# Top-k attention with a feed-forward block: the scores of a row folded in two before the top 32 are selected

## The chip, the cores and the metric

The kernel runs on one core of a Trainium2 chip. The metric is the device time of one execution in microseconds (us). The core has five engines that work side by side, each with its own queue in program order: TensorE (PE, matrix products and transposes), VectorE (DVE), ScalarE (ACT), GpSimd (POOL) and SyncE (SP, which here only issues transfers). They wait for each other through semaphores.

## The reference

```python
scores = scale * np.matmul(q, k.transpose(0, 1, 3, 2))     # (8, 8, 576, 576), head_dim 64
kth = np.partition(scores, -32, axis=-1)[..., -32:-31]     # the 32nd largest of each row
scores = np.where(scores >= kth, scores, -1e9)
attn = softmax(scores)                                      # with 1e-9 added to the sum
x = np.matmul(attn, v)                                      # -> (4608, 512)
h = x @ w_in                                                # 512 -> 2048
g = np.where(h > 0, h, np.exp(np.minimum(h, 0)) - 1)        # ELU
out = g @ w_out                                             # 2048 -> 512
```

For each of 36,864 rows of 576 scores the kernel needs the largest score and the 32nd largest.

## The kernel before, in words

The attention work is cut into 144 steps. A step is one tile of 128 queries for a pair of heads: two score rows of 576 in every partition, `u.sc[:, i, :]` for i = 0 and 1. The main loop (L702) emits the pieces of several steps in one hand-written order, with a manual schedule from step 8 on (L729), so each engine's queue is exactly the order of the code. In iteration n:

- PE and ACT make the scores of step n+2 (`scores`, L322: matmuls at L331, and ACT scales them out of PSUM at L339).
- DVE selects for step n (`select`, L366). MAX8 gives the eight largest values of a row in order; MATCH_REPLACE8 overwrites those eight with -1e30, and the next MAX8 gives the next eight. Four MAX8 (L373, L385) and three MATCH_REPLACE8 (L378) for each row, all over 576 scores, leave the largest in `u.first` and the 32nd largest in `u.last[..., 7]`. The first eight steps use `select_row` (L344), the same passes in another order. `select` is a generator with four parts; the other work is emitted between its parts.
- `mask` (L389) is for step n-1: POOL computes `gap`, the 32nd minus the largest (L406), ACT maps the scores under the threshold far away (a steep Prelu, L407) and takes the exponential with `gap` as bias, with the row sum going into `den` (L408). Row 0 is emitted after the first part of the selection, row 1 after the third.
- `turn` (L429) is for step n-2: PE transposes the probabilities (L444), ACT copies them to `et` (L445). `attend` multiplies with v (L470) and ACT copies the result into `xT` (L497).
- `normalise` (L412), last in the iteration, is again for step n-1: on POOL five small instructions make the reciprocal of the row sums (L418 to L423), and two multiply the score rows by it (L425). So POOL's queue holds, for each step: normalise of step n-1, then (from iteration n+1) `gap` of step n, then normalise of step n.
- `feed` (L661), four times in an iteration, adds pieces of the feed-forward block of tokens that are ready, by a written cost list: `hidden(f)` (L532: eight matmul records at L545, then ACT: the two ReLUs at L555 and L558, the exponential at L560 and a subtraction of one at L564) and `project` (L567: matmuls at L573). A block holds one, two or three 128-token slots. The last addition of ELU, called a gate, is queued up and later done by POOL (L515), or by DVE (L517) near the start and in the last block.

The weights come as 64-bit floats and are decoded to 32 bits in the first steps (`decode_piece`, L211; its integer addition on POOL is L193). When the last piece is done, `hook` (L199) closes the pools of the decoding and opens those of the main part, in the dictionary `late`.

Of the kernel before, what the change touches and what calls it, by code (L numbers as in the profile page):

```python
# [7 lines left out]

AF = mybir.ActivationFunctionType
ALU = mybir.AluOpType  # L10
FP32 = mybir.dt.float32
U32 = mybir.dt.uint32
I32 = mybir.dt.int32
# [3 lines left out]
TOP_K = 32  # L17
TAKEN = -1.0e30
# [63 lines left out]
def kernel(  # L82
# [9 lines left out]
    nc = tc.nc  # L92
    P = nc.NUM_PARTITIONS
    B, H, S, D = q.shape
# [4 lines left out]
    HS = S // 2  # L99
# [4 lines left out]
    T = 3 * P  # L104
# [7 lines left out]
    def pool(name, bufs, **kw):  # L112
        return ctx.enter_context(tc.tile_pool(name=name, bufs=bufs, **kw))
# [4 lines left out]
    wkpool = pool("wk", 1)  # L118
    etpool = pool("et", 2)
    small = pool("small", 4)  # L120
# [2 lines left out]
    ps_sc = pool("ps_sc", 1, space=PSUM)  # L123
    ps_t = pool("ps_t", 2, space=PSUM)
    ps_f = pool("ps_f", 2, space=PSUM)
    wide = [ps_sc.tile([P, 2, JP], FP32, tag=f"s{i}", name="scps") for i in range(2)]
    late = {}
    raws = ExitStack()
# [33 lines left out]
    def convert_first(i):  # L162
# [10 lines left out]

        ef = parts(raw[i])[1].bitcast(FP32)
        top = (2.0 - 2.0**-3 - 2.0**-23) * 2.0**16
        nc.gpsimd.tensor_scalar(ef, ef, top, -top, ALU.min, ALU.max)

# [9 lines left out]
    def convert_third(i):  # L187
        lo = parts(raw[i])[0]
        nc.vector.tensor_single_scalar(lo, lo, 3, ALU.logical_shift_left)

    def convert_last(i):
        w, t = weight(i)[1].bitcast(I32), raw.pop(i)
        nc.gpsimd.tensor_tensor(w, w, parts(t)[0].bitcast(I32), ALU.add)  # L193

# [4 lines left out]
    def hook():  # L199

        if not decode:
            return
        decode.pop(0)()
        if not decode:
            raws.close()
            late["f"] = ctx.enter_context(tc.tile_pool(name="f", bufs=2))
            late["g"] = ctx.enter_context(tc.tile_pool(name="g", bufs=2))
            late["x"] = ctx.enter_context(tc.tile_pool(name="xt", bufs=2))
            late["in"] = ctx.enter_context(tc.tile_pool(name="in", bufs=2))
# [134 lines left out]
    def select_row(u, i, decoding):  # L344
        if i == 0:
            u.first = small.tile([P, 2, 8], FP32, tag="m1", name="m1")
            u.last = small.tile([P, 2, 8], FP32, tag="m4", name="m4")
        sc = u.sc[:, i, :]
        m = u.first[:, i, :]
        nc.vector.max(m, sc)  # L350
        wk = wkpool.tile([P, S], FP32, tag=f"wk{i}", name="wk")
        cur = sc
        for r in range(TOP_K // 8 - 1):
            nc.vector.match_replace(wk[:], m, cur, TAKEN)
            cur = wk[:]
            if r < TOP_K // 8 - 2:
                m = small.tile([P, 8], FP32, tag=f"m{i}", name="m")[:]
            else:
                m = u.last[:, i, :]
            nc.vector.max(m, cur)  # L360
            if r > 0 and decoding:
                hook()
            if r != 1:
                yield

    def select(u):  # L366

        u.first = small.tile([P, 2, 8], FP32, tag="m1", name="m1")
        u.last = small.tile([P, 2, 8], FP32, tag="m4", name="m4")
        cur = [u.sc[:, i, :] for i in range(2)]  # L370
        found = [u.first[:, i, :] for i in range(2)]
        for i in range(2):
            nc.vector.max(found[i], cur[i])  # L373
        yield
        wk = [wkpool.tile([P, S], FP32, tag=f"wk{i}", name="wk")[:] for i in range(2)]
        for r in range(TOP_K // 8 - 1):
            for i in range(2):
                nc.vector.match_replace(wk[i], found[i], cur[i], TAKEN)  # L378
            cur = wk
            for i in range(2):  # L380
                if r < TOP_K // 8 - 2:
                    found[i] = small.tile([P, 8], FP32, tag=f"m{i}", name="m")[:]
                else:
                    found[i] = u.last[:, i, :]
                nc.vector.max(found[i], cur[i])  # L385
            hook()
            yield

    def mask(u, i, early=False):  # L389

# [130 lines left out]
    def ffn_pieces(blk):  # L521
        n_tok = blk.slots * P
        bank = dm // n_tok
        unit = max(2, bank)

        def hidden(f):
            if f == 0 and blk.number == 0:
                g = early.tile([P, NF, P], FP32, tag="g", name="gT")
                blk.gT = [g[:, 0:NG], g[:, NG:NF]]
            elif f % NG == 0 and blk.number > 0:  # L530
                g = late["g"].tile([P, NG, T], FP32, tag="g", name="gT")
                blk.gT.append(g[:])  # L532
            if f % unit == 0:
                if len(gates) > 1:
                    close_gates(upto=gates[0][1])
                if blk.number == 0:
                    n = earlyf.tile([P, 4 * P], FP32, tag="n", name="n")
                else:
                    n = late["f"].tile([P, 2 * T], FP32, tag="n", name="n")
                blk.n = n[:, 0 : unit * n_tok].rearrange("p (f t) -> p f t", f=unit)  # L540
            if f % bank == 0:
                ps = ps_f.tile([P, dm], FP32, tag="f", name="hps")
                blk.h = ps[:, 0 : bank * n_tok].rearrange("p (f t) -> p f t", f=bank)
            for i in range(NC):
                nc.tensor.matmul(  # L545
                    blk.h[:, f % bank, :],
                    w_in[:, i, f * P : (f + 1) * P],
                    blk.xT[:, i, 0:n_tok],
                    start=(i == 0),
                    stop=(i == NC - 1),  # L550
                )
            g, end = blk.gT[f // NG], f % NG + 1
            if end % bank == 0:
                n0 = f % unit + 1 - bank
                nc.scalar.activation(  # L555
                    blk.n[:, n0 : n0 + bank, :], blk.h, AF.Relu, scale=-1.0
                )
                nc.scalar.activation(g[:, end - bank : end, 0:n_tok], blk.h, AF.Relu)  # L558
            if end % unit == 0:
                nc.scalar.activation(blk.n, blk.n, AF.Exp, scale=-1.0)  # L560
                dst = g[:, end - unit : end, 0:n_tok]
                apart = place[0] > 4 * (tight + 3) and blk is not blocks[-1]
                if apart:
                    nc.scalar.activation(blk.n, blk.n, AF.Copy, bias=-1.0)  # L564
                gates.append((place[0], (blk.number, f + 1 - unit), dst, blk.n, apart))

        def project(s, part):  # L567
            close_gates(upto=(blk.number, (part + 1) * NF // 4 - 1))
            if part == 0:
                blk.o = ps_f.tile([P, dm], FP32, tag="f", name="ops")  # L570
            step = NF // 4
            for f in range(part * step, (part + 1) * step):
                nc.tensor.matmul(  # L573
                    blk.o[:],
                    blk.gT[f // NG][:, f % NG, s * P : (s + 1) * P],
                    w_out[:, f, :],
                    start=(f == 0),
                    stop=(f == NF - 1),
                )
            if part == 3:  # L580
                o = opool.tile([P, dm], FP32, tag="osb", name="osb")
                nc.scalar.copy(o[:], blk.o[:])
                for t in blk.tiles[s]:
                    p0 = t.cols.start - s * P
                    nc.sync.dma_start(out[t.rows, :], o[p0 : p0 + t.ql, :])

        part = HIDDEN[blk.slots]
        behind = 2 * NF if blk.number else 0
        return [
            (part, max(behind, NC * (f // 4 + 1)), lambda f=f: hidden(f))  # L590
            for f in range(NF)
        ] + [
            (PROJECT, max(behind, NF + (part + 1) * NF // 4),
             lambda s=s, part=part: project(s, part))
            for s in range(blk.slots)
            for part in range(4)
        ]
# [4 lines left out]
    for b in range(B):  # L602
        if b % 2 == 0:
            rest = 2 * J
# [4 lines left out]
            for part in division:  # L609
                blk = Block(len(blocks), len(part))  # L610
# [20 lines left out]
        for qts in order:  # L631
# [3 lines left out]
            for qt in qts:  # L635
                n = len(steps)
# [12 lines left out]
    for b in range(1, B):  # L649
        f = first[b]  # L650
# [50 lines left out]
    main, rest, other = slice(0, J), slice(J, J + 1), slice(J + 1, 2 * J + 1)  # L701
    for n in range(NS + 3):  # L702
        for fn, args in todo.pop(n, []):
            fn(*args)
        ahead, cur, prev, done = step(n + 2), step(n), step(n - 1), step(n - 2)
        if n < tight:
# [5 lines left out]
            for i in range(2):  # L712
                passes = select_row(cur, i, n < tight - 1)
# [13 lines left out]
            continue  # L727
        if n == tight:
            ctx.enter_context(tc.manual_schedule(engines=engines))  # L729
        passes = select(cur) if cur else iter(range(4))  # L730
        if ahead and n > tight:
            scores(ahead)
        while closing:
# [58 lines left out]
```

## Time and profile before

Three runs gave 1637.93, 1642.47 and 1644.79 us; the median is 1642.47. The profiled execution has a span of 1640.8 us from the first to the last instruction, 1.7 us under that median.

| what | value |
|---|---|
| median of the runs | 1642.47 us |
| span of the profiled execution | 1640.8 us |
| mean granted TensorE clock | 0.974 of full speed |
| DVE, scans L373, L378, L385 | 191.6 + 401.4 + 200.6 + 577.9 us |
| POOL, normalise and gates (L425, L515) | 213.0 + 164.9 us |
| ACT, Prelu and exponential (L407, L408) | 225.3 + 223.6 us |
| transfers, mean rate | 34 GB/s |

The busy time of an engine is the union of its instructions; a matmul's end is modelled, so PE at 96% is not proof of PE at its peak. The weight loads (PEld) run beside the matmuls. A row of the groups gives line, engine, operation, tiles, shapes and count, then the busy time and the mean of one, then how long the engine was idle just before and what ended that. The stages of the execution differ: the decoding of the weights fills about the first 160 us, the selections run from there to 1520 us, and what is left of the feed-forward block ends the execution.

### The profile page before, as it was taken

Reading aid. Unit: us, or ns where it says so; the run is one execution under the profiler, and the core shown is the slowest. Engines: PE = TensorE matmul, PEld = TensorE weight load, DVE = VectorE, ACT = ScalarE, POOL = GpSimd, SP = SyncE. Lnnn points to the kernel's source line nnn. Section 1 sums busy time; section 2 is a strip of 40 time slices with the busy share of each in tenths; the row PEclk is TensorE's granted clock in tenths of the full one; section 3 lists DMA queues with packets and bytes.
Section 4 is the critical chain, followed back from the end, with each engine's and each line's share of the span. In section 5 each row is a group of like instructions: output and inputs, shape, how many; then the busy total and the mean of one; then the engine's idle time right before and its main releaser. Section 6 shows DMA issues by size and latency. Waiting matters only on the chain.

```text
span 1640.8 us, 25344 instructions
## 1 busy us (share of the span) xinstructions
PE 1581.7 (96%) x8276; PEld 1011.8 (62%) x8276; DVE 1453.4 (89%) x2981; ACT 1187.7 (72%) x2400; POOL 708.7 (43%) x1534
## 2 busy tenths in 40 slices
PE   4788999999999999999999999999999999999999
PEld 3566777666575757555566666655557575755564
DVE  6987999999999999999999699999999599998000
ACT  6887778778695867778678686868759595958521
POOL 4775445445353534445335353535435353534300
PEclk8579999999999999999999999999999999999999
DMA  7431221012100310012100211012100201000000
GB/s 226 151 128 25 50 40 26 7 22 45 42 1 7 59 42 8 7 22 44 36 14 15 43 30 28 1 28 44 36 14 0 43 1 35 1 13 2 7 13 14
DMA packets 188037, 56.18 MB, mean 34 GB/s; under 512 B 178177, under 2 KB 179201, under 8 KB 187905
## 3 DMA queue, kind: packets, MB, share of 16 engines
q1 hardware_dynamic: 186704, 54.26, 14.1%
q8 instruction: 66, 1.08, 0.3%
q14 instruction: 67, 0.54, 0.1%
q10 hardware_dynamic: 1200, 0.30, 0.1%
HBM read 45.09 MB, written 9.44 MB: 33 GB/s over the span
## 4 chain that ended last, share of the span: by engine, by line
PE 76%; ACT 12%; DVE 7%; POOL 3%; issue 1%; DMA 1%; SPq 0%; ACTq 0%; DVEq 0%; POOLq 0%
PE ops L573 29%; PE hps L545 23%; PE avps L470 10%; PE scps L331 7%; PE eps L444 6%; DVE wk L378 3%; DVE m L385 3%; ACT sc L408 2%; ACT et L445 2%; ACT sc L407 2%; DVE m L373 1%; ACT n L564 1%; ACT n L555 1%; ACT sc L339 1%; ACT n L560 1%
## 5 line engine op out<-in xcount | busy, mean ns | idle before, releaser
L385 DVE MAX8 m<-wk 128x8 f32<-128x576 f32 x816 | 577.9, 752 | 0.3 <-POOL den L406 0.3
L545 PE MATMUL hps<-xT,w_in 128*128 128x256 f32 (+2 forms) x2432 | 545.8, 374 | 0.0
L573 PE MATMUL ops<-w_out,gT 128*128 128x512 f32 x1152 | 523.6, 599 | 0.0
L545 PEld LDWEIGHTS hps<-xT,w_in 128*128 128x128 f32 x2432 | 406.0, 192 | 100.1 <-issue 26.3
L378 DVE MATCH_REPLACE8 wk<-m,wk 128x576 f32<-128x576 f32 x544 | 401.4, 748 | 0.0
L573 PEld LDWEIGHTS ops<-w_out,gT 128*128 128x128 f32 x1152 | 209.0, 190 | 233.9 <-issue 232.8
L418 POOL TENSOR_SCALAR dene<-den 128x2 f32<-128x2 f32 x144 | 32.9, 228 | 686.5 <-ACT sc L408 686.1
L408 ACT ACTIVATE sc<-sc,den 128x576 f32<-128x576 f32 x288 | 223.6, 776 | 65.5 <-POOL den L406 44.2
L407 ACT ACTIVATE sc<-sc,m 128x576 f32<-128x576 f32 x288 | 225.3, 782 | 10.8 <-DVE m L385 10.7
L470 PE MATMUL avps<-et,vT 128*64 128x256 f32 (+2 forms) x2080 | 207.2, 330 | 17.4 <-ACT et L445 17.2
L425 POOL TENSOR_SCALAR sc<-sc,rec 128x576 f32<-128x576 f32 x288 | 213.0, 750 | 15.0 <-POOL rec L423 0.2
L331 PE MATMUL scps<-kqT 64*128 64x288 f32 (+1 forms) x1280 | 206.0, 442 | 13.6 <-ACT kqT L307 9.1
L339 ACT ACTIVATE sc<-scps 128x576 f32<-128x576 f32 x288 | 171.8, 647 | 65.1 <-PE scps L331 65.1
L445 ACT COPY et<-eps 128x512 f32<-128x512 f32 x288 | 164.6, 571 | 73.4 <-PE eps L444 73.4
L378 DVE MATCH_REPLACE8 wk<-m,sc 128x576 f32<-128x576 f32 x272 | 200.6, 748 | 0.0
L373 DVE MAX8 m<-sc 128x8 f32<-128x576 f32 x272 | 191.6, 749 | 8.8 <-ACT sc L339 8.8
L444 PEld LDWEIGHTS eps<-ident,sc 128*128 128x128 f32 x1152 | 144.9, 144 | 87.2 <-issue 52.7
L444 PE MATMUL eps<-ident,sc 128*128 128x128 f32 x1152 | 177.1, 279 | 13.7 <-POOL sc L425 13.7
L470 PEld LDWEIGHTS avps<-et,vT 128*64 128x64 f32 x2080 | 128.5, 142 | 98.8 <-ACT et L445 31.7
L515 POOL TENSOR_TENSOR gT<-n,gT 128x512 f32<-128x512 f32 (+1 forms) x119 | 164.9, 1386 | 31.2 <-ACT n L564 31.1
L331 PEld LDWEIGHTS scps<-kqT 64*128 64x128 f32 (+1 forms) x1280 | 111.3, 182 | 89.5 <-issue 43.8
L555 ACT ACTIVATE n<-hps 128x512 f32<-128x512 f32 (+1 forms) x156 | 87.3, 559 | 56.8 <-PE hps L545 56.0
(53 smaller groups left out, 1089.6 us busy)
## 6 DMA issues: line engine op xcount, KB each, us to landing
raw<-in_moe_w_in_dram SPq DMA_DIRECT2D x16, 512.0 KB, 6.1
vT<-in_v_dram SPq DMA_DIRECT2D x64, 128.0 KB, 2.5
raw<-in_moe_w_out_dram SPq DMA_DIRECT2D x16, 512.0 KB, 3.6
out_dram<-osb SPq DMA_DIRECT2D x32, 256.0 KB, 2.1
kin<-in_k_dram SPq DMA_DIRECT2D x112, 72.0 KB, 2.5
qin<-in_q_dram SPq DMA_DIRECT2D x112, 72.0 KB, 2.6
kin<-in_k_dram SPq DMA_DIRECT2D x8, 128.0 KB, 4.5
vT<-in_v_dram SPq DMA_DIRECT2D x64, 16.0 KB, 2.2
```

Of the source, the lines that this page charges most:

```text
L331: nc.tensor.matmul(wide[i][rows, half, 0:HS], kq[part, q0 : q0 + u.t.ql], kq[part, k0 : k0 + HS], start=True, stop=True,)
L373: nc.vector.max(found[i], cur[i])
L378: nc.vector.match_replace(wk[i], found[i], cur[i], TAKEN)
L385: nc.vector.max(found[i], cur[i])
L407: nc.scalar.activation(sc, sc, AF.Prelu, scale=-1.0, bias=low, alpha=1.0 / STEEP)
L408: nc.scalar.activation(sc, sc, AF.Exp, scale=-STEEP, bias=gap, accum_out=u.den[:, i : i + 1])
L425: nc.gpsimd.tensor_scalar(u.sc[:, i, :], u.sc[:, i, :], rec[:, i : i + 1], 1.0, ALU.mult, ALU.mult)
L444: nc.tensor.transpose(ps[:, c * P : (c + 1) * P], sc[:, c0 : c0 + P], ident[:])
L445: nc.scalar.copy(g.et[:, chunks, u.at, :], ps[:, 0 : n * P].rearrange("p (c q) -> p c q", c=n),)
L470: nc.tensor.matmul(ps[i * D : (i + 1) * D, cols], vt[:, 2 * J + i if c == J else i * J + c, :], w, start=(c == 0), stop=(c == J),)
L545: nc.tensor.matmul(blk.h[:, f % bank, :], w_in[:, i, f * P : (f + 1) * P], blk.xT[:, i, 0:n_tok], start=(i == 0), stop=(i == NC - 1),)
L573: nc.tensor.matmul(blk.o[:], blk.gT[f // NG][:, f % NG, s * P : (s + 1) * P], w_out[:, f, :], start=(f == 0), stop=(f == NF - 1),)
```

## The change

For every step after the decoding, `select` is replaced by `select_folded`. Both rows of 576 scores are treated as two halves of 288 that are compared element by element. DVE writes the larger of each pair to `high`. POOL adds the two halves as 32-bit integers, bit pattern by bit pattern, and subtracts `high` as an integer, which leaves exactly the bit pattern of the smaller: `low`. DVE then takes the 32 largest of `high` (four MAX8 and three MATCH_REPLACE8 over 288) and the 16 largest of `low` (two MAX8 and one MATCH_REPLACE8 over 288). The 32nd largest of the whole row is found by a join: with a rank list of each, the larger of `high`'s 32nd value and the pairwise minima of `high`'s 16th to 31st and `low`'s 16th to 1st (a minimum over 2x16 values, and a maximum reduction).

`wk`, which held the working copies of the two rows, becomes one tile: its first half holds the rest of `high` for both rows, its second half `low`. `high` has one buffer, the lists have three. To make room, blocks of three slots close a gate for each f (384 wide) where they closed one for two (768 wide).

```diff
+    wk = wkpool.tile([P, 2, S], FP32, tag="wk", name="wk")
...
+            late["high"] = ctx.enter_context(tc.tile_pool(name="high", bufs=1))
+            late["top"] = ctx.enter_context(tc.tile_pool(name="top", bufs=3))
...
+    def select_folded(u):
+
+        one, other = u.sc[:, :, 0:HS], u.sc[:, :, HS:S]
+        high = late["high"].tile([P, 2, HS], FP32, tag="high", name="high")
+        rest, low = (
+            wk[:, i, :].rearrange("p (a s) -> p a s", a=2) for i in range(2)
+        )
+        found = late["top"].tile([P, 2, TOP_K], FP32, tag="found", name="found")
+        second = late["top"].tile([P, 2, TOP_K // 2], FP32, tag="second", name="second")
+        u.first = found
+        u.last = small.tile([P, 2, 8], FP32, tag="m4", name="m4")
+        nc.vector.tensor_tensor(high[:], one, other, ALU.max)
+        nc.gpsimd.tensor_tensor(
+            low.bitcast(I32), one.bitcast(I32), other.bitcast(I32), ALU.add
+        )
+        nc.gpsimd.tensor_tensor(
+            low.bitcast(I32), low.bitcast(I32), high[:].bitcast(I32), ALU.subtract
+        )
+        for i in range(2):
+            nc.vector.max(found[:, i, 0:8], high[:, i, :])
+        yield
+        cur = high
+        for r in range(0, TOP_K - 8, 8):
+            for i in range(2):
+                nc.vector.match_replace(
+                    rest[:, i, :], found[:, i, r : r + 8], cur[:, i, :], TAKEN
+                )
+            cur = rest
+            for i in range(2):
+                nc.vector.max(found[:, i, r + 8 : r + 16], rest[:, i, :])
+            if r < TOP_K - 16:
+                yield
+        for i in range(2):
+            nc.vector.max(second[:, i, 0:8], low[:, i, :])
+        for i in range(2):
+            nc.vector.match_replace(low[:, i, :], second[:, i, 0:8], low[:, i, :], TAKEN)
+        for i in range(2):
+            nc.vector.max(second[:, i, 8:16], low[:, i, :])
+        pairs = found[:, :, TOP_K // 2 - 1 : TOP_K - 1]
+        nc.vector.tensor_tensor(pairs, pairs, second[:, :, ::-1], ALU.min)
+        nc.vector.tensor_reduce(
+            u.last[:, :, 7:8], found[:, :, TOP_K // 2 - 1 : TOP_K], AX.X, ALU.max
+        )
+        yield
...
-        unit = max(2, bank)
+        unit = max(2, bank) if blk.slots < 3 else 1
...
-                    n = late["f"].tile([P, 2 * T], FP32, tag="n", name="n")
+                    n = late["f"].tile([P, 4 * P], FP32, tag="n", name="n")
...
-        passes = select(cur) if cur else iter(range(4))
+        choose = select_folded if late else select
+        passes = choose(cur) if cur else iter(range(4))
```

133 steps are folded. The order of PE's queue stays as it was. On POOL the two integer instructions of step n+1 come right after the normalise of step n-1 (a gate stands between them in some steps), and so ahead of the `gap` of step n.

More of the change, by code (lines that the diff above doesn't have):

```diff
@@ L10 @@
 ALU = mybir.AluOpType
+AX = mybir.AxisListType
 FP32 = mybir.dt.float32
@@ L350, in select_row @@
         nc.vector.max(m, sc)
-        wk = wkpool.tile([P, S], FP32, tag=f"wk{i}", name="wk")
         cur = sc
         for r in range(TOP_K // 8 - 1):
-            nc.vector.match_replace(wk[:], m, cur, TAKEN)
-            cur = wk[:]
+            nc.vector.match_replace(wk[:, i, :], m, cur, TAKEN)
+            cur = wk[:, i, :]
             if r < TOP_K // 8 - 2:
@@ L374, in select @@
         yield
-        wk = [wkpool.tile([P, S], FP32, tag=f"wk{i}", name="wk")[:] for i in range(2)]
         for r in range(TOP_K // 8 - 1):
             for i in range(2):
-                nc.vector.match_replace(wk[i], found[i], cur[i], TAKEN)
-            cur = wk
+                nc.vector.match_replace(wk[:, i, :], found[i], cur[i], TAKEN)
+            cur = [wk[:, i, :] for i in range(2)]
             for i in range(2):
```

## The prediction

> **What bounds the kernel now.** I read the page's totals and its chain first, then busy time by stretch, then the waits, then the timeline of single steps. The totals and the chain:
>
> ```profile
> PE 1581.7 (96%) x8276; PEld 1011.8 (62%) x8276; DVE 1453.4 (89%) x2981; ACT 1187.7 (72%) x2400; POOL 708.7 (43%) x1534
> ...
> PE 76%; ACT 12%; DVE 7%; POOL 3%; issue 1%; DMA 1%; SPq 0%; ACTq 0%; DVEq 0%; POOLq 0%
> ```
>
> POOL looks idle. By stretch (busy us of PE, PEld, DVE, ACT, POOL, then the granted clock):
>
> ```profile
> 500.00:700.00 200.00, 196.29 (x1098) 125.24 (x1097) 200.00 (x413) 147.08 (x300) 84.82 (x198) 1.00 0.12 25
> 900.00:1100.00 200.00, 200.00 (x1112) 127.53 (x1110) 185.77 (x383) 144.63 (x294) 83.71 (x196) 1.00 0.14 28
> ```
>
> ```profile
> 1404.93:1416.05 11.12, 11.12 (x69) 8.59 (x65) 11.12 (x23) 9.90 (x21) 5.77 (x11) 1.00 0.00 0
> 1416.05:1426.30 10.25, 10.25 (x58) 8.26 (x57) 10.25 (x23) 9.52 (x20) 5.77 (x11) 1.00 0.01 2
> ```
>
> In 500 to 700 DVE is full and PE has 3.7 us left; in 900 to 1100 PE is full and DVE waits. So a lighter DVE can win only what PE leaves idle. The second fence is two single steps of the kind that carries ELU pieces: ACT is at 9.5 to 9.9 us of 10.3 to 11.1. The waits (us in total, times, longest):
>
> ```profile
> POOL dene L418 <- ACT sc L408: 686.1, 139, 12.8
> ...
> ACT sc L408 <- POOL den L406: 44.2, 49, 4.3
> ```
>
> POOL's idle time is nearly all one wait, for the exponential; and 49 times ACT waits for POOL's gap. They close a loop, seen in the second step above, POOL first and then ACT:
>
> ```profile
> 1416.38 0.23 POOL L418 TENSOR_SCALAR dene<-den 128x2 f32<-128x2 f32 x1 [4.91 <-ACT sc L408]
> ...
> 1418.35 1.48 POOL L425 TENSOR_SCALAR sc<-sc,rec 128x576 f32<-128x576 f32 x2
> 1419.79 1.27 POOL L515 TENSOR_TENSOR gT<-n,gT 128x512 f32<-128x512 f32 x1
> 1421.02 0.19 POOL L406 TENSOR_TENSOR den<-m,m 128x1 f32<-128x1 f32 x1
> ```
>
> ```profile
> 1421.24 0.78 ACT L408 ACTIVATE sc<-sc,den 128x576 f32<-128x576 f32 x1 [0.58 <-POOL den L406]
> ...
> 1424.79 0.79 ACT L407 ACTIVATE sc<-sc,m 128x576 f32<-128x576 f32 x1
> 1425.66 0.78 ACT L408 ACTIVATE sc<-sc,den 128x576 f32<-128x576 f32 x1
> 1426.34 0.19 ACT L408 ACTIVATION_READ_ACCUMULATOR sc<-sc,den 128x1 f32 x1
> ```
>
> Normalise 3.5 us, gate 1.2, gap 0.2, exponential of row 0, ELU pieces and copies, exponential of row 1, next normalise: 10.24 us without a hole.
>
> **The change part by part.**
>
> *POOL, two integer instructions in that loop.* Nearest rows: the integer addition over 512 has a median of 1.28 to 1.30 us; the float gates take 1.28 us for 512 and 1.82 for 768, so 2.1 ns per element and 1.41 for 576. Two: 2.82, with hand-over 2.9 us, 133 times: 386 us of busy time that would fit in POOL's idle 932 us. But they stand between normalise(n-1) and gap(n). POOL's queue runs in order, which makes gap, the exponential of row 0 and all behind it on ACT (ReLUs, the copies of the transposes) 2.9 us later wherever the gap is awaited. Bounds: 2 x 1.28 = 2.6 to 2 x 1.76 (slowest integer row) = 3.5. The pair has waits of its own, for DVE: the addition for DVE's last read of the previous `low`, the subtraction for `high`. Around 1400 DVE runs some 17 us ahead of the exponentials, so both are met; early they are met about when the gap's own wait for DVE is (25.7 us in 32 times), and that wait is merely moved ahead of the pair.
>
> By the timeline, the gap's end and the start of row 0's exponential are under 0.1 us apart in 49 of the 133 steps, under 1 us in 81, and 2.9 us or more in 28. Take the nine steps from 1227.40 to 1320.83. Five carry ELU pieces (the 9.76 us step that starts this kind, 11.1, 10.25, 11.1, 8.1: together 50.3 us). Their slack (from gap to exponential, or later on ACT waiting for PE's hidden piece, 0.76 at 1411.75) is 0.8, 0.5, 0, 0.5 and 0 us, so the loop grows by 2.1 + 2.4 + 2.9 + 2.4 + 2.9 = 12.7. The steps of projections (12.6, 7.6, 13.2, then round again) have a loop of 3.5 + 2.9 + 0.2 + 0.9 + 2.3 = 9.8 against a mean over 10 us: PE bounds them, they neither lose nor give back. Recovery: PE can run ahead of the late ReLUs by the second of its two PSUM banks for the hidden layer; one bank is 16 records of L545, 3.65 us in the chain around 1408. Net 9.1 us a block of two slots.
>
> Blocks: ten of two slots lie inside the selection: 91. Three of three slots have, in their seven steps, four whose slack is under 2 us, which add 2.3 + 1.4 + 1.2 + 2.9 = 7.8, less one bank of 2.7 and about 1 us that longer steps between take up: 4 each, 12. Five of one slot lie early, where steps follow DVE at 9.6 to 9.9 us; there the loop of 9.8 does not show, but the 1.2 us gate on top of it does, in two or three steps a block: 3 each, 15. Sum 118.
>
> *Unit of one f in three-slot blocks.* ACT's L560 and L564 go from 24 x 0.84 each to 48 of 384 wide; the ReLUs of that width take 0.486: 2 x 24 x (0.972 - 0.845) = 6 us in ACT, within the slack of those steps. POOL: 188 ns more for each of 24 gates, 4.5 us. Bounds 0 to 10; I take 0.
>
> *DVE.* MAX8 pairs start 0.66 us apart and MATCH_REPLACE8 0.72 (with its value load), so a step is 8 x 0.66 + 6 x 0.72 = 9.6 us. For 288, the value load of eight elements (0.06 to 0.08) shows how little a short instruction costs: (0.66 + 0.07)/2 = 0.365, and 0.42 with the load. New step: 12 x 0.365 + 8 x 0.42 + pairwise maximum 0.78 (L517, 0.693 alone over 512) + join 0.5 = 9.0. Ends: half of 0.66, with a join of 0.3, 8.2; no saving beyond the 0.15 us tail that a 0.75 us MAX8 shows, 0.45 a scan, 10.9. DVE saves 0.6 us a step and, with the loop near 11.3, buys nothing: its cover is that loop. If DVE alone were what holds PE, the gain would end at PE's idle time between 164 and 900 us, 2.7 + 4.6 + 3.7 + 1.6 = 12.6 us in four stretches.
>
> *Low is also awaited by DVE* at the seventh scan pair: 0.8 + 0.7 + 4.7 = 6.2 us into its step; behind it stand the join, the next step's pairwise maximum and the key transposes L285. POOL delivers 3.5 + 2.9 us after the exponential (1.3 more with a gate), DVE then needs 2.8: done 9 to 10.5 us into a loop of 10 to 13. DVE's lead shrinks but stays over one step. 0.
>
> *The shared port.* L517 took 0.693 us alone and 1.08 to 1.63 beside POOL's two-input instructions. DVE's maximum can be stretched by 0.4 to 0.9; hidden as above. SBUF — State Buffer in the Trainium skill, section "SBUF: two separate sides", says more: a DVE instruction with two SBUF inputs and a GpSimd one that reads SBUF lock each other out for a whole instruction. It agrees with the 1.63, and speaks against this change: were POOL's pair blocked by one maximum every step, 0.78 x 133 = 104 us would be an estimate of the addition, and the sum 1865. I expect the maximum to fall in POOL's gap-to-exponential idle time instead.
>
> *SP, PE.* No new transfers; PE's order is unchanged. 0.
>
> Sum: 1640.8 + 118 = 1759 in the profiled execution, 1.7 below the median: 1761.
>
> **The rivals.**
>
> (A) *PE hides the loop, and DVE's relief shows: faster.* For it: PE fills 96% and its chain share is 76%. It decides if POOL's pair adds less than the gap's spare time in the ELU steps, 0 to 0.8 us instead of 2.9. Then 1640.8 - 12.6 = 1628, 1630 by the median. Against: the rows at 1421.24.
>
> (B) *Smaller loss.* PE's run-ahead is two banks (7.3 us) and the pair takes 2.6: ten blocks of 11.2 - 7.3 = 4, others 10: 1640.8 + 50 + 1.7 = 1692. For it: the slack between the end of a normalise and its transposes, 1408.7 to 1411.7, is not used above.
>
> (C) *The clock falls too.* PE would idle about 7%; with PE 78% busy from 41 to 82 us the granted clock was 0.50, against 1.00 when full. At 0.92 the 1340 us of selection stage hold 1340 x 0.08 = 107 us more of PE work, some half of it in the idle time: +55, 1816. TensorE: Matmul & The Clock Gate (Trainium skill, section "HAM oscillation — how this bites in real kernels") would ask for idle gaps of some 3.4 us; here each is under 3, so by it the clock stays.
>
> (D) *DVE becomes the bound.* Scans of 0.45, both two-input instructions stretched by 0.5: 11.9 us a step against 10.2: 133 x 1.7 = 226, 1868.
>
> **How the numbers follow.** The forecast case (1715 to 1800) has 0.54; B, 1665 to 1715, 0.14; C, to 1850, 0.13; D 0.10; A 0.05; no change 0.04. Likeliest 1761. The range 1675 to 1845 leaves out A, no change, most of D and an edge of B and C. Half a per cent, 8 us, is about what can be told from no change; faster 0.05, same 0.04, slower 0.91 by the same cases.
>
> **What would show it.** POOL busy near 1100 us; ACT's wait for the gap from 44 us to 250 or more; PE's busy digits 9 falling in ELU steps only, which lengthen to 12 to 13.5 us while projection steps stay; DVE's scans near 0.45 long, 0.37 apart, its total some 1380, with a new wait for `wk` from POOL. Wrong if ACT's wait stays small, if DVE is full, or if the clock leaves 1.00.

## The result: 9% slower

The changed kernel takes 1794.2 us (median of 4 runs, 1791.23 to 1795.76), the kernel before on the same chip 1641.8. The ratio is 1.0922, with a 95% interval of 1.0901 to 1.0942. The profiled execution has a span of 1792.7 us, 151.9 more than the 1640.8 of before. The totals and the chain of the kernel after:

```profile
PE 1662.3 (93%) x8276; PEld 1051.7 (59%) x8276; DVE 1366.3 (76%) x4444; ACT 1184.0 (66%) x2448; POOL 1085.0 (61%) x1824
...
POOL 30%; PE 27%; ACT 19%; DVE 19%; issue 4%; SPq 0%; DMA 0%; POOLq 0%; ACTq 0%; DVEq 0%
```

DVE became 87 us lighter and POOL 376 us heavier. No engine is full over the span, and POOL's share of the chain went from 3% to 30%. By stretch, and for the two steps that answer to those shown of before (the same place in the same block of two slots):

```profile
500.00:700.00 200.00, 185.13 (x1020) 119.84 (x1018) 167.48 (x566) 135.10 (x277) 130.35 (x222) 0.98 0.12 24
900.00:1100.00 200.00, 191.22 (x1029) 122.48 (x1025) 158.25 (x536) 131.26 (x268) 125.45 (x215) 0.98 0.12 24
```

```profile
1538.17:1551.29 13.12, 12.54 (x69) 9.37 (x69) 8.70 (x32) 9.79 (x21) 8.56 (x13) 1.00 0.00 1
1551.29:1564.40 13.11, 10.20 (x49) 7.93 (x49) 8.99 (x33) 9.52 (x20) 8.54 (x13) 0.96 0.01 2
```

The steps went from 11.12 and 10.25 us to 13.1. PE, DVE and ACT all have holes in the second. The waits (us in total, times, longest) and the groups that bear on them:

```profile
POOL dene L465 <- ACT sc L455: 496.6, 139, 9.6
ACT sc L455 <- POOL den L453: 310.6, 102, 7.3
DVE second L424 <- POOL wk L406: 290.6, 119, 10.1
...
PE scps L335 <- ACT et L492: 47.0, 31, 3.6
```

```profile
L406 POOL TENSOR_TENSOR wk<-wk,high 128x576 int32<-128x576 int32 x133 | 186.8, 1404 | 10.4
...
L403 POOL TENSOR_TENSOR wk<-sc 128x576 int32<-128x576 int32 x133 | 187.3, 1408 | 0.0
```

ACT waits for POOL's gap (L453 here) 310.6 us where it waited 44.2. DVE has a new wait of 290.6 us for `low`. Which of the two carries the loss is not told by their sizes, and is left to the experiments. POOL and ACT in the second of the two steps, from the timeline:

```profile
1551.62 0.23 POOL L465 TENSOR_SCALAR dene<-den 128x2 f32<-128x2 f32 x1 [4.04 <-ACT sc L455]
...
1555.04 1.27 POOL L562 TENSOR_TENSOR gT<-n,gT 128x512 f32<-128x512 f32 x1
1556.27 1.41 POOL L403 TENSOR_TENSOR wk<-sc 128x576 int32<-128x576 int32 x1
1557.76 1.40 POOL L406 TENSOR_TENSOR wk<-wk,high 128x576 int32<-128x576 int32 x1
1559.12 0.19 POOL L453 TENSOR_TENSOR den<-m,found 128x1 f32<-128x1 f32 x1
```

```profile
1555.14 0.78 ACT L454 ACTIVATE sc<-sc,m 128x576 f32<-128x576 f32 x1
1559.34 0.78 ACT L455 ACTIVATE sc<-sc,den 128x576 f32<-128x576 f32 x1 [3.43 <-POOL den L453]
```

The queue runs normalise, gate, the two new instructions, gap, without a hole; ACT stands still for 3.43 us in front of the exponential, and behind it in ACT's queue stand the ReLUs and copies that PE waits for.

To see where the 152 us lie, I took from both timelines the end of row 1's exponential of every step and compared step lengths. Steps 114 to 122 of before are the nine that the prediction worked with:

| step | 114 | 115 | 116 | 117 | 118 | 119 | 120 | 121 | 122 |
|---|---|---|---|---|---|---|---|---|---|
| before, us | 9.76 | 11.12 | 10.25 | 11.12 | 8.09 | 12.61 | 7.55 | 13.16 | 9.77 |
| after, us | 11.88 | 13.11 | 13.10 | 13.10 | 10.94 | 11.06 | 9.72 | 11.06 | 11.89 |

Five of the nine steps after have the length of the loop to a tenth: 13.1 with a gate and hidden pieces (three of them), 10.9 with a gate, 9.7 with neither. In the two of 11.06 us PE is busy for 10.8 and 11.1 us; the two of 11.9 us begin a run of ELU steps.

### The profile page after: what moved, and what is told of

It reads as the page before. It is cut to its first block, busy times and chain, and to the rows that moved or that the text cites. A ratio compares the mean times of both kernels' runs of the same rounds, so it can differ in the third digit from the quotient of the medians.

```text
span 1792.7 us, 27164 instructions
## 1 busy us (share of the span) xinstructions
PE 1662.3 (93%) x8276; PEld 1051.7 (59%) x8276; DVE 1366.3 (76%) x4444; ACT 1184.0 (66%) x2448; POOL 1085.0 (61%) x1824
## 4 chain that ended last, share of the span: by engine, by line
POOL 30%; PE 27%; ACT 19%; DVE 19%; issue 4%; SPq 0%; DMA 0%; POOLq 0%; ACTq 0%; DVEq 0%
PE ops L620 14%; POOL sc L472 7%; POOL wk L406 7%; ACT sc L455 7%; POOL wk L403 7%; PE avps L517 5%; PE hps L592 5%; DVE wk L415 4%; ACT sc L454 3%; POOL gT L562 3%; ACT et L492 3%; DVE found L420 3%; POOL rec L467 2%; PE scps L335 2%; DVE wk L426 2%
## 5 line engine op out<-in xcount | busy, mean ns | idle before, releaser
L592 PE MATMUL hps<-xT,w_in 128*128 128x256 f32 (+2 forms) x2432 | 553.2, 378 | 0.8 <-ACT gT L605 0.7
L455 ACT ACTIVATE sc<-sc,den 128x576 f32<-128x576 f32 x288 | 223.5, 776 | 326.9 <-POOL den L453 310.6
L424 DVE MAX8 second<-wk 128x8 f32<-128x288 f32 x266 | 109.0, 452 | 290.8 <-POOL wk L406 290.6
L420 DVE MAX8 found<-wk 128x8 f32<-128x288 f32 x798 | 323.5, 447 | 0.0
L335 PE MATMUL scps<-kqT 64*128 64x288 f32 (+1 forms) x1280 | 242.0, 455 | 57.8 <-ACT et L492 47.0
L517 PE MATMUL avps<-et,vT 128*64 128x256 f32 (+2 forms) x2080 | 240.9, 353 | 40.2 <-ACT et L492 39.7
L415 DVE MATCH_REPLACE8 wk<-found,wk 128x288 f32<-128x288 f32 x532 | 231.5, 443 | 0.0
L517 PEld LDWEIGHTS avps<-et,vT 128*64 128x64 f32 x2080 | 148.5, 152 | 138.2 <-ACT et L492 63.5
L335 PEld LDWEIGHTS scps<-kqT 64*128 64x128 f32 (+1 forms) x1280 | 125.2, 185 | 152.4 <-ACT et L492 67.2
L406 POOL TENSOR_TENSOR wk<-wk,high 128x576 int32<-128x576 int32 x133 | 186.8, 1404 | 10.4
L403 POOL TENSOR_TENSOR wk<-sc 128x576 int32<-128x576 int32 x133 | 187.3, 1408 | 0.0
```

What stands on the lines that cost most here:

```text
L335: nc.tensor.matmul(wide[i][rows, half, 0:HS], kq[part, q0 : q0 + u.t.ql], kq[part, k0 : k0 + HS], start=True, stop=True,)
L403: nc.gpsimd.tensor_tensor(low.bitcast(I32), one.bitcast(I32), other.bitcast(I32), ALU.add)
L406: nc.gpsimd.tensor_tensor(low.bitcast(I32), low.bitcast(I32), high[:].bitcast(I32), ALU.subtract)
L415: nc.vector.match_replace(rest[:, i, :], found[:, i, r : r + 8], cur[:, i, :], TAKEN)
L420: nc.vector.max(found[:, i, r + 8 : r + 16], rest[:, i, :])
L455: nc.scalar.activation(sc, sc, AF.Exp, scale=-STEEP, bias=gap, accum_out=u.den[:, i : i + 1])
```

## The experiments

### The pair moved behind the gaps

```diff
-        nc.gpsimd.tensor_tensor(low, one, other, ALU.add)        # as integers
-        nc.gpsimd.tensor_tensor(low, low, high, ALU.subtract)
...
         for r in range(0, TOP_K - 8, 8):
+            if r == 8:
+                nc.gpsimd.tensor_tensor(low, one, other, ALU.add)
+                nc.gpsimd.tensor_tensor(low, low, high, ALU.subtract)
```

> The folded kernel with one thing moved: POOL's integer addition and subtraction for the next step are emitted in the third part of the selection, so that in POOL's queue they come after both gaps of the step before and not ahead of them. Same instructions, same data. Theory of the loop (normalise, pair, gap, exponential): the 2.9 us leave the loop and run while POOL waits for the exponential, so ACT's wait for the gap falls from 311 us to under 80 and the time falls to 1625 to 1655 us. Rival 1, DVE's new wait for low (291 us in all) or its two-input instructions are what costs: that wait stays at 200 us or more, and the time stays over 1740. Rival 2, POOL's load itself (61% busy) slows ACT and DVE by contention: over 1740 too.

Measured: 1659.68 us, 1.0099 times the kernel before (1.0082 to 1.0116). That is 16 us over the kernel before of the same rounds (1643.58), so of the 152 us 136 are gone by moving the two instructions behind the two gaps in POOL's queue, with the same instructions on every engine. The waits of this kernel:

```profile
POOL dene L466 <- ACT sc L456: 306.8, 127, 10.8
...
DVE second L425 <- POOL wk L412: 142.3, 63, 8.4
...
ACT sc L456 <- POOL den L454: 62.7, 53, 4.5
```

The pair now lies in the time in which POOL waits for the exponential (686 us before, 307 here). Contention as the main cause is out: POOL is busier here (1128 us) than in the changed kernel. It was expected at 1625 to 1655 and came out 5 us over; the runs below look at the rest of 16 us. DVE's wait for `low` halved with it, so this run alone does not yet part the two waits.

### The scans of before, with the pair added

```diff
+            nc.gpsimd.tensor_tensor(low, one, other, ALU.add)      # into a tile that nobody reads
+            nc.gpsimd.tensor_tensor(low, low, one, ALU.subtract)
         cur = [u.sc[:, i, :] for i in range(2)]                    # select(), 576 scores
```

> The kernel before (its scans over 576, nothing folded, with the one-f unit), with the two POOL instructions of the change added at the same place in POOL's queue: they add the halves of the score rows and subtract one again into a tile that nobody reads. DVE neither waits for them nor has less to do. Theory of the loop: nearly the whole loss is there, 1770 to 1815 us, and ACT waits about 300 us for the gap. Rival, the loss comes through DVE (its wait for low, then the gap's wait for DVE): 1640 to 1680.

Measured: 1792.11 us, 1.0907 (1.0881 to 1.0932): the whole loss without folding (the unit of one f is in this kernel too). Its chain and ACT's wait:

```profile
PE 33%; POOL 32%; ACT 28%; issue 4%; DMA 1%; DVE 1%; SPq 1%; ACTq 0%; POOLq 0%; DVEq 0%
...
```

```profile
ACT sc L414 <- POOL den L412: 298.8, 101, 7.3
```

Here DVE never waits for `low`, has its old 14 scans a step, and stands in 1% of the chain; what it waits for instead is POOL's gap, 117 us in two rows of the waits (`m` L391 and L379). So the loss does not need DVE's wait for `low`, which was 291 us in the changed kernel. That kernel, with its lighter DVE, is 2 us slower than this one and the two intervals overlap: no gain of the lighter DVE is to be seen.

### The gap made by ACT

```diff
-            mask(prev, 0)
+            mask(prev, 0, True)
...
-            mask(prev, 1)
+            mask(prev, 1, True)
```

> The folded kernel, POOL's pair where the change put it, but the gap made by ACT (as in the first eight steps of the kernel), so that the exponential no longer waits for POOL. Theory: the gap is the only link by which the pair reaches the path; without it the loss goes, less 0.6 us more ACT a step, which shows where ACT is full: 1655 to 1695 us. Rival, the pair also hurts through the next normalise or through the wait for low: over 1740.

Measured: 1680.56 us, 1.0245 (1.0225 to 1.0266). The pair stays where the change put it, and it is 40 us over the kernel before of its rounds (1640.36): 112 of the 152 us go once the exponential no longer waits for POOL. The gap is the link. The rest holds the 12 us of the next but one experiment and ACT's 61 us of extra work, which shows in the early steps (+10.5 us in steps 9 to 30) and in the three-slot blocks.

### The smaller half made by DVE

```diff
-        nc.gpsimd.tensor_tensor(low, one, other, ALU.add)        # as integers
-        nc.gpsimd.tensor_tensor(low, low, high, ALU.subtract)
+        nc.vector.tensor_tensor(low, one, other, ALU.min)
```

> The folded kernel with the smaller half made by DVE, as one minimum of the two halves in place of POOL's two integer instructions; POOL's queue is then that of the kernel before. DVE carries 0.75 us more a step, about 9.7 us, as much as before the change. Theory of the loop: 1635 to 1660 us, ACT's wait for the gap near the 44 us of before. Rival, the folded selection on DVE costs by itself (twenty scans with a fixed part, joins, two-input instructions beside POOL): over 1700.

Measured: 1670.24 us, 1.0164 (1.0149 to 1.0179), 10 us over the upper end. ACT waits 53.6 us for the gap, near the 44.2 of before. So the loss without the pair is the 12 us of the unit and some 14 more, of which 7 lie in steps 31 to 65, where DVE sets the pace. The two-input instructions of DVE took 838 and 849 ns in the mean in this kernel, up to 1.8 us, where the maximum of the changed kernel took 748. Beside them POOL's gap, mostly 0.19 us, was stretched by 0.1 us or more in 95 of 266 cases, 46 us in all. How much of the 14 us either makes was not tried apart.

### The unit of one f alone

```diff
-        unit = max(2, bank)
+        unit = max(2, bank) if blk.slots < 3 else 1
```

on the kernel before.

> The kernel before, with only the last part of the change: blocks of three slots make and close their gates for one f at a time. By the prediction this is 6 us of ACT and 4.5 us of POOL off the path: within 5 us of the kernel before. Rival, it is what made the three-slot blocks lose 28 us in all where 12 were predicted: 10 to 20 us slower than before.

Measured: 1655.66 us, 1.0078 (1.0063 to 1.0093): 12 us slower, as the rival had it; in the profiled execution 13.0. All of it lies in the three blocks of three slots (step by step against before: +5.0, +6.7 and +3.3 us, 15.0 in sum, while the first nine steps came out 2.2 us shorter). ACT in one of them, and PE's wait behind it:

```profile
745.63 0.47 ACT L555 ACTIVATE n<-hps 128x384 f32<-128x384 f32 x1
746.00 0.48 ACT L558 ACTIVATE gT<-hps 128x384 f32<-128x384 f32 x1
746.37 0.52 ACT L560 ACTIVATE n<-n 128x384 f32<-128x384 f32 x1
746.92 0.52 ACT L564 ACTIVATE n<-n 128x384 f32<-128x384 f32 x1
747.35 0.57 ACT L445 COPY et<-eps 128x512 f32<-128x512 f32 x1
...
755.47 0.37 ACT L497 COPY xT<-avps 128x256 f32<-128x256 f32 x1 [2.46 <-PE avps L470]
```

```profile
751.97 3.46 PE L470 MATMUL avps<-et,vT 128*64 128x256 f32 x18 [2.02 <-ACT et L445]
```

ACT has no hole for ten microseconds. With two f in a unit, the exponential and the subtraction come after every second pair of ReLUs; now each hidden piece brings all four, so the copies of the transposes behind them come later and PE waits for one of them at 751.97 (2.02 us). The price was not ACT's 6 us in all, but where they fell.

A part of it came by way of TensorE's clock. In two of the steps that grew (69 and 105) this wait of 2.02 us is followed by 3.4 us at half clock. Step 69 without such a window, in the run with one POOL instruction (below), and with it, here (length of the step, busy us of PE, PEld, DVE, ACT and POOL, then the granted clock):

```profile
762.06:777.02 14.96, 12.94 (x62) 7.66 (x61) 11.67 (x40) 10.85 (x26) 8.13 (x15) 1.00 0.23 42
```

```profile
749.63:766.22 16.59, 14.57 (x62) 8.39 (x61) 16.59 (x34) 10.83 (x25) 6.49 (x14) 0.90 0.30 53
```

PE's wait of 2.02 us stands in both; the 18 matmuls behind it take 2.37 us in the first run and 3.46 in the second. The step is 1.6 us longer with the window, so the two windows are some 3 of the 15 us, an estimate from this pair.

### One and three instructions ahead of the gap

```diff
-        nc.gpsimd.tensor_tensor(low, one, other, ALU.add)        # as integers
-        nc.gpsimd.tensor_tensor(low, low, high, ALU.subtract)
+        nc.gpsimd.tensor_tensor(low, one, other, ALU.subtract)   # as floats: one instruction
```

> The folded kernel with one POOL instruction of 1.4 us in place of the two, at the same place (a float subtraction of the halves, so the smaller half and the output are not the reference's). Theory of the loop: it is 1.45 us shorter in every step; the ELU steps of two-slot blocks then lose some 4 us a block and the projection steps nothing, which with the 12 us of the unit gives 1680 to 1720 us, ACT's wait for the gap 120 to 200 us. Rival, a fixed cost of having any POOL work ahead of the gap: over 1760.

```diff
+        nc.gpsimd.tensor_tensor(low, one, other, ALU.add)        # a third: the addition twice
         nc.gpsimd.tensor_tensor(low, one, other, ALU.add)
         nc.gpsimd.tensor_tensor(low, low, high, ALU.subtract)
```

> The folded kernel with the integer addition done twice, so three POOL instructions ahead of the gap. Theory of the loop: with three even the projection steps (9.7 us in the loop with two, 11.2 with three, against 10.8 of PE's work) are held by it, so nearly all of 1.45 x 133 = 193 us comes on top: 1930 to 1990 us. Rival, POOL's busy time is hidden but for one wait: under 1880.

Measured: 1688.87 us with one (1.0296), 1969.37 us with three (1.2006). ACT's wait for the gap:

```profile
ACT sc L450 <- POOL den L448: 145.0, 87, 5.9
```

```profile
ACT sc L458 <- POOL den L456: 456.9, 118, 8.8
```

The three stand at 12 (the unit alone), 49, 152 and 329 us over before for none, one, two and three instructions. Each adds 1.4 to 1.5 us to the loop, but the increments are 37, 103 and 177 us. The first lands mostly in slack; the third is paid in nearly every one of the 133 steps (177/133 = 1.33). A wait that is hidden has a price of nothing up to its slack and its full length from there on.

### The pair behind the gaps, with the old unit

```diff
-        unit = max(2, bank) if blk.slots < 3 else 1
+        unit = max(2, bank)
...
         for r in range(0, TOP_K - 8, 8):
+            if r == 8:            # high has been read: the smaller half takes its place
+                nc.gpsimd.tensor_tensor(high, one, high, ALU.subtract)   # as integers
+                nc.gpsimd.tensor_tensor(high, high, other, ALU.add)
```

> The folded kernel with POOL's pair after both gaps (as in the run before that moved it), and with the three-slot blocks' unit of two f as in the kernel before. To make room, the smaller half is made in place of high, once the first replacement has read it. Both known costs are out: 1659.7 less the 12 us of the unit, 1640 to 1652 us. Were DVE's lighter step worth anything, it would show here as a time under 1640; the theory that PE holds the pace says it does not.

Measured: 1648.13 us, 1.0047 (1.0033 to 1.0061). Both costs are out, DVE is 69 us lighter than in the kernel before, and the time is still 8 us over it. So folding does not pay in this kernel even with both costs out. 74 of the 113 steps from 31 on keep their length of before to 0.05 us, though DVE has less to do in each, and from 700 to 1500 us PE is busy for 198 to 199.4 of every 200: PE holds the pace there. In the profiled execution the rest is 6 us, and one thing that makes it is seen in a step that grew by 0.57 us (step 132). POOL in the normalise, and DVE beside it:

```profile
1422.15 0.72 POOL L467 TENSOR_TENSOR rec<-dene,power 128x2 f32<-128x2 f32 x1
1422.94 0.77 POOL L468 TENSOR_TENSOR dene<-dene,rec 128x2 f32<-128x2 f32 x1
1423.81 0.19 POOL L469 TENSOR_SCALAR dene<-dene 128x2 f32<-128x2 f32 x1
```

```profile
1422.91 0.75 DVE L400 TENSOR_TENSOR wk<-sc 128x576 f32<-128x576 f32 x1
```

L468 works on two elements a partition and takes 0.20 us in most steps. Here it ends with DVE's maximum, which began 0.03 us before it. Whether that is all of the 6 us was not tried apart.

## Why the prediction was right

The terms of its sum against the step lengths of both traces (us):

| term of the sum | predicted | measured | where |
|---|---|---|---|
| ten blocks of two slots | 91 | 101 | steps 31-65, 74-101, 110-136 |
| three blocks of three slots, the loop | 12 | 13 | 28.1 less the unit (taken as adding up) |
| five blocks of one slot, early | 15 | 23 | up to step 30 |
| unit of one f | 0 | 15 | the unit alone, by its steps, some 3 of it through the clock |
| sum | 118 | 152 | |

**The loop.** Right, and shown from four sides: moving the pair takes the loss away, adding it to the old scans brings all of it, cutting its one link does nearly as well as moving it, and one and three instructions give what the loop's length says. The pair's price of 2.9 us was 2.85: steps without slack grew by 2.84 to 2.87.

**Two-slot blocks.** The sum was near for partly wrong reasons. The five ELU steps grew by 11.8 us, not 12.7, since the steps of 11.1 us had 0.87 of slack. The 3.65 us of run-ahead through the second PSUM bank are not to be seen. In their place the projection steps gave back 1.5 us a round (7.55 to 9.72, but 12.61 and 13.16 to 11.06), which the prediction had ruled out. Errors of opposite sign stand in this term, so it is in part luck that it came within 10 us.

**Unit of one f.** This is the term of the sum that failed: "I take 0", with "within the slack of those steps", and bounds of 0 to 10. It was 12 us by the medians and 15 by steps, outside those bounds. These are ELU steps, whose ACT the prediction itself had shown nearly full; its busy time was added up, and the order in which it stands before the copies that PE waits for was not looked at.

**Early blocks.** 23 for 15. DVE set the pace there before, and a loop of 9.8 (9.7 when measured) was taken to be hidden behind 9.6 to 9.9 us; steps of 8.1 to 8.8 us were among them, and in these it was not.

**DVE.** MAX8 over 288 takes 0.447 us and two of them start 0.37 apart, two of MATCH_REPLACE8 0.43; 0.365 and 0.42 had been worked out from the value load. That a lighter DVE buys nothing held, in the runs with the old scans and with the old unit. Its wait for `low` was put at no cost, and the run with the old scans shows none.

**The port.** In the changed kernel the maximum took 716 to 759 ns in all 133 steps: it falls mostly into POOL's idle time, as taken. The lock that the Trainium skill describes (SBUF — State Buffer, "SBUF: two separate sides") agrees with the rows just shown, where a POOL instruction waited for all of a DVE maximum. In the kernel as changed only five small POOL instructions were stretched like this (0.69 to 0.81 us in place of 0.19 to 0.23); in the first run with the pair moved, 88 were.

**The rivals.** (A) is out: DVE's relief shows in no run. (B) took a longer run-ahead, there was hardly any. (C) is in part right, and one sign that the prediction had named for being wrong, a clock that leaves 1.00, did come. The granted clock fell from 0.974 to 0.956, by 18 windows at half speed in the folded steps where the kernel before has one. The prediction kept the clock at 1.00 because PE's gaps would stay under 3 us, and that step failed: 17 of the 18 windows follow a PE wait of 1.7 to 2.8 us, and only one a longer wait (3.6). So the limit of some 3.4 us that it drew on is not what this case shows. Where the loop sets the length of a step, a window costs nothing: steps 96 and 97 took 13.10 us, the second with a window in it. Elsewhere it costs. Step 105 in the changed kernel, without a window, and in the run with the old scans, with one:

```profile
1236.72:1251.68 14.96, 13.70 (x68) 7.90 (x65) 10.18 (x34) 10.85 (x26) 9.29 (x16) 1.00 0.15 30
```

```profile
1236.46:1253.10 16.64, 14.62 (x62) 8.33 (x61) 14.50 (x29) 10.84 (x26) 9.27 (x16) 0.90 0.17 32
```

Four steps of the changed kernel (31, 69, 139 and 141) are 0.8 to 1.7 us longer with a window than in a run without one. By these the clock makes some 6 of the 152 us, an estimate, in place of the 55 that (C) had for it.

(D) is out: DVE waits for POOL, 76% busy.

## What to carry to other kernels

An engine that is idle for more than half of the time may still have none to give at one point of its queue: before putting work on it, follow what stands behind the new instruction there and who waits for that. Where a loop runs over several engines (here POOL's normalise and gap, ACT's exponentials, POOL again), its length per step is compared with the pace of the bound engine, step kind by step kind; work inside it is free up to the slack and then costs its full length each time. And a small change that only makes room can cost as much as a term of the sum, if it reorders the queue of an engine that is full in that stage.

## What had not been expected of the hardware

Two-input instructions of DVE and small instructions of POOL met in the kernels with the moved pair: a POOL multiplication of two elements a partition took 0.77 us in place of 0.20 beside a DVE maximum of 0.75, and DVE's own join of 32 elements took up to 1.19 us in place of 0.19. In the kernel as changed such meetings were fewer, because the longer loop leaves POOL idle at that moment in most steps: five small POOL instructions were stretched, and the join once to 1.23 us.

TensorE's granted clock went to half for single windows of 3.4 us (6.8 us at times) about once in seven folded steps after the change, mostly behind PE waits of only 2.0 to 2.8 us, and to a mean of 0.922 with three instructions ahead of the gap, where PE was still 89% busy.
